# W_in's first two word blocks issued by ScalarE at the start, and 1e-9 added to the first 16 heads' sums by GpSimd

## The chip, the cores and the metric

One core of one Trainium2 chip. Five engines run their own instruction streams: TensorE (matrix products), VectorE, ScalarE, GpSimd and SyncE, which here only issues DMAs. The metric is the device time of one execution in microseconds, the median of several runs. The profile names the engines PE (and PEld for its weight loads), DVE, ACT, POOL and SP; a q behind a name is that engine's queue of issues.

## The reference

Attention with a decay, then two layers of a wide network, all in float32. Four batches, eight heads, 576 tokens, 64 elements in a head; 2304 tokens, width 512, inner width 2048.

```python
log_f = np.log(np.clip(f, 0.0001, 1.0))
cum = np.cumsum(log_f, axis=-1)
scores = scale * np.matmul(q, k.transpose(0, 1, 3, 2))
scores = np.where(causal, -1e9, scores + cum[..., :, None] - cum[..., None, :])
attn = np.exp(scores - np.max(scores, axis=-1, keepdims=True))
attn = attn / (np.sum(attn, axis=-1, keepdims=True) + 1e-09)
x = np.matmul(attn, v)                     # 2304 x 512 after merging the heads
h = x @ w_in;  x = np.maximum(0.01 * h, h) @ w_out
h = x @ w_in2; y = h / (1 + np.exp(-h)) @ w_out2
```

## The kernel before

The attention runs over 64 pieces that the code calls heads: each of 4 batches is cut into its first 256 and its last 320 tokens, and each half has 8 heads, so heads 0 to 7 are the first half of batch 0, and 8 to 15 its second half. The queries of a head are cut into blocks of at most 128 rows, two in a first half, three in a second.

For one block, `score` issues the product of queries and keys on TensorE (line 744; for heads 0 and 1 lines 735 and 737), the mask and row minimum on VectorE (`least`, line 724), and the exponential with its row sum on ScalarE (line 767). `shares` (line 782) then waits for the exponentials of all blocks of the head, adds 1e-9 to the sums on VectorE (line 786) and takes the reciprocal there (line 787). Each block is scaled by it on VectorE (line 775) or ScalarE (line 777). TensorE transposes the blocks (`transp`, line 825), they are copied out of PSUM (lines 359 and 360), and after every second head `weigh` multiplies both with the values (line 893) and writes the result into the ring, from which the next layer reads. The scores of head n+1 are issued before the transposes of head n, and those of head n+2 after them.

Beside the attention, W_in is made ready. The weights lie in HBM as pairs of 32-bit words; 16 blocks of 128 x 512 elements, 512 KB of words each. `fetch` (line 1745) takes a room for a block and issues its DMA; `conv_in` (line 1757) decodes the block with `to_f32`: one instruction on ScalarE (line 1714), three on VectorE (1715, 1716, 1718), then a rounded copy on ScalarE (line 359) and the remainder by a subtraction on VectorE (line 374, into tile w). Three lines of `conv_in` run beside each other. When heads 0 to 7 are through, the products with W_in begin (lines 961 and 1055, `hps` and `hpw`) and share TensorE with the later heads.

The order on each engine is worked out before the kernel runs, by a planner (class `Plan`). The parts of the kernel are generators; each step names an engine, an estimated duration, a rank and a delay. Whenever the planner's clock finds an engine free, it issues the waiting step of the lowest rank, and the order found in this way is the program. Attention steps have rank 0, decode steps rank 1, DMAs of later words rank 2. A step on another engine, another estimate or another wait thus changes the order of everything behind it. While TensorE has no step ready, and until the first product with W_in is complete in the plan, the planner puts filler products on it (lines 461, 464 and 466, tile `fps`).

Before the change all words are issued by SyncE. The blocks 0 and 1 (`EARLY` is 2) get a rank between the small DMAs that carry the cumulated logarithms into the key tiles of heads 2 to 7 (`first_rows`, line 540). `first_weights` starts with a wait for `cf`, the copy of these logarithms, and for `v0_sent`, the issue of the values' DMA; the blocks from 2 on wait for `rows` as well. The inputs of the very first steps are f (lines 474 and 476, clamped on GpSimd in line 398, logarithm on ScalarE in line 480) and the queries and keys of heads 0 and 1 (lines 598 and 600); one of the latter is issued by ScalarE, the rest by SyncE. GpSimd builds masks and constants until some 8 us, and takes subtractions of the later heads (line 370) from 74 us on.

Of the kernel before, what the change touches and what calls it, by code (L numbers as in the profile page):

```python
# [11 lines left out]
I32 = mybir.dt.int32  # L12
ACTF = mybir.ActivationFunctionType
ALU = mybir.AluOpType
# [20 lines left out]
DIRECT = 2  # L35
EARLY = 2
# [52 lines left out]
class Plan:  # L89
# [41 lines left out]
    def op(self, eng, cost, fn, rank=1, lat=None):  # L131
        def step(resume):
            self.count += 1
            heapq.heappush(self.ready.setdefault(eng, []), (rank, self.count, cost, fn, lat, resume))
            self.at(self.now, lambda: self.issue(eng))

        return step
# [39 lines left out]
    def dma(self, nbytes, fn, rank=1):  # L177
        return self.op("sp", 0.64, fn, rank, nbytes / self.rate)

    def wait(self, *names):  # L180
        def step(resume):
            missing = [n for n in names if n not in self.seen]
            if not missing:
                resume()
                return
            left = [len(missing)]

            def one():
                left[0] -= 1
                if not left[0]:  # L190
                    resume()

            for n in missing:
                self.waiting.setdefault(n, []).append(one)

        return step
# [8 lines left out]
    def signal(self, name):  # L205
        self.seen[name] = True
        for fn in self.waiting.pop(name, []):
            fn()
# [13 lines left out]
    def give(self, pool, i):  # L222
        self.given[pool, i] = True
        fn = self.queue.pop((pool, i), None)
        if fn:
            fn()
# [20 lines left out]
    def par(self, *gens):  # L247
        def step(resume):
            left = [len(gens)]

            def one():
                left[0] -= 1
                if not left[0]:
                    resume()

            for g in gens:
                self.start(g, one)

        return step
# [11 lines left out]
def dve_cost(n, fast=False):  # L271
    return 0.07 + n * (0.52e-3 if fast else 1.042e-3)
# [15 lines left out]
def fused_kernel(ctx, tc, qt, kt, va, vb, ft, w1, wi2, wo2, out):  # L288
    nc = tc.nc
    B, H, _, S = qt.shape  # L290
    D = va.shape[-1]
    NT, DM = out.shape
# [11 lines left out]
    p = Plan()  # L304
    op, dma, wait, take, give, signal, par = p.op, p.dma, p.wait, p.take, p.give, p.signal, p.par
# [44 lines left out]
    def dve(n, fn, rank=1, fast=False):  # L350
        return op("dve", dve_cost(n, fast), fn, rank)
# [228 lines left out]
    def head_info(n):  # L580
        sb, h = divmod(n, H)
        return sb // 2, sb % 2, h

    def plain(n):

        return n < PLAIN
# [114 lines left out]
    def score(n, i):  # L701
# [10 lines left out]
        if i == 0:  # L712
            ht["i_st"] = yield take("st", ST_BUFS)
            p.start(shares(n, stats[ht["i_st"] % ST_BUFS]))
# [67 lines left out]
    def shares(n, st):  # L782

        nb = len(BLOCKS[head_info(n)[1]])
        yield wait(*[("exp", n, i) for i in range(nb)])
        yield dve(1, lambda: nc.vector.tensor_scalar(st[:, 6:6 + nb], st[:, 6:6 + nb], 1e-9, None, op0=ALU.add), 0)
        yield dve(1, lambda: nc.vector.reciprocal(st[:, 9:9 + nb], st[:, 6:6 + nb]), 0)
        signal(("shares", n))
        yield wait(*[("p", n, i) for i in range(nb)])
        give("st", heads[n]["i_st"])  # L790
# [273 lines left out]
    def tagged(k, shape, dtype, name):  # L1064
        return w2t["a"].tile(shape, dtype, tag=f"x{k}", name=name)
# [661 lines left out]
    def room(f):  # L1727

        where = ROOM_IN[f]
        shape = [128, DM, 2]  # L1730
        name, bufs = (where, {"ring0": RING_BUFS, "ring1": RING_BUFS, "g": G_BUFS, "stg": STG_BUFS}.get(where, 1))
        if isinstance(where, int):
            name = ("w", where)
        i = yield take(name, bufs)
        if where in ("ring0", "ring1"):
            t = main.tile(shape, I32, tag=where, name="wsr", bufs=RING_BUFS)
        elif where == "g":
            t = main.tile(shape, I32, tag="g", name="wsg", bufs=G_BUFS)
        elif where == "stg":
            t = stg(i, shape, I32, "wst")  # L1740
        else:
            t = slot(where, shape, I32, "wss")
        return t, lambda: give(name, i)

    def fetch(f):
        t, back = yield from room(f)

        def move():
            yield dma(524e3, lambda: nc.sync.dma_start(
                out=t.rearrange("p n w -> p (n w)"), in_=w1[f, :, 0:DM].bitcast(I32)),  # L1750
                2 if f >= EARLY else DIRECT // 2 - H + 0.5)
            words[f] = t, back
            signal(("words", f))

        p.start(move())
# [24 lines left out]
    def fetch_out():  # L1780
        yield wait("gates")
        for j in range(FF // 2):
            for e in range(2):
                i_s = yield take("wst", WST_BUFS)
                src = decp["wo"].tile([128, DM, 2], I32, tag="wst", name="wst", bufs=WST_BUFS)
                words1[j, e] = src, i_s

                def move(j, e, src):
                    yield dma(524e3, lambda: nc.sync.dma_start(
                        out=src.rearrange("p n w -> p (n w)"), in_=w1[j + e * FF // 2, :, DM:2 * DM].bitcast(I32)), 2)  # L1790
                    signal(("words1", j, e))

                p.start(move(j, e, src))

    def conv_out():
        out_d = w2_d[0].rearrange("p (s f) n -> p s f n", s=7)
        for j in range(FF // 2):
            yield wait(("words1", j, 0))
            i_f = yield take("wf", 1)
            f = decp["wo"].tile([128, 7, HW], F32, tag="wf", name="wf", bufs=1)  # L1800
            y = f[:, 4:6].rearrange("p s n -> p (s n)")
            for e in range(2):
                yield wait(("words1", j, e))
                src, i_s = words1.pop((j, e))
                t = f[:, 2 * e:2 * e + 2].rearrange("p s n -> p (s n)")
                yield from to_f32(t, src, y, t, 2, True)
                give("wst", i_s)
            yield from mix(f, 1, 2)
            yield dma(918e3, lambda: nc.sync.dma_start(out=out_d[:, :, j], in_=f), 2)
            give("wf", i_f)  # L1810
            signal(("spilt", 0, j))

    def first_weights():
        def fetches():
            for f in range(FF):
                if f == EARLY:
                    yield wait("rows")
                yield from fetch(f)

        def line(fn, todo):  # L1820
            while todo:
                yield from fn(todo.pop(0))

        yield wait("cf", "v0_sent")
        ins = list(range(FF))
        yield par(fetches(), *[line(conv_in, ins) for _ in range(C_LINES)])
        signal("weights")
        yield wait(("scored", OUT_AT, 0))
        p.start(fetch_out())
        yield from conv_out()  # L1830
        yield wait("attention")
        wo_es.close()
        w2t["a"] = ctx.enter_context(tc.tile_pool(name="w2a", bufs=1, side="right"))
        for k in range(6):
            w2t["q", k] = tagged(k, [128, 2, 2, TB], F32, "gq")
        for k in range(SPLITS):
            w2t["s", k] = tagged(6 + k, [128, 2, 2, TB], F32R, "gs")
        w2t["b"] = ctx.enter_context(tc.tile_pool(name="w2b", bufs=1))
        signal("decoded")
# [133 lines left out]
    with tc.manual_schedule():  # L1973
        for gen in (opening(), first_weights(), loads(), attention(), hidden(), quarters(), preps(), summed(), all_fills(),
                    second_input(), second_weights(), hidden2(), second_values(), summed2()):
            p.start(gen)
        p.run()
# [51 lines left out]
```

## Time and profile before

| | |
|---|---|
| median of 3 runs | 952.9 us (951.85 to 955.81) |
| the profiled execution | 955.32 us, span 953.6 us, granted TensorE clock 0.998 |
| PE busy | 938.0 us, 98% of the span |
| DVE busy | 758.0 us, 79% |
| ACT busy | 612.1 us, 64% |
| POOL busy | 53.7 us, 6% |
| chain that ended last, by engine | PE 80%, DVE 9%, DMA 4%, ACT 3%, issue 2%, SPq 1% |
| DMA | 196.77 MB, mean 206 GB/s |

Busy shares are means over the whole span. The change touches the first tenth of it, so the rows below are mostly of that part. The span runs from the first to the last instruction; the execution's own time has a little more around it. PE's busy time is modelled and includes the fillers.

### The profile page before, as it was taken

To read this page: it belongs to the slowest core of one execution; us is meant where nothing else is said; L and a number is where in the kernel's file an instruction comes from. 1 tells how busy PE (TensorE), PEld (TensorE's weight loads), DVE (VectorE), ACT (ScalarE), POOL (GpSimd) and SP (SyncE) were. 2 spreads that over 40 slices of the span, in tenths; PEclk is the share of its full clock that TensorE was granted. 3 is DMA by queue.
4 is the path that set the end of the run, shared out by engine and by line. 5 is a ranking of instruction groups with operands and counts; after the bars stand their busy time and mean duration, and the time that the engine had idled before them with its cause. 6 is when DMAs were issued, how large, how long until landed. Compare 5 with 4: busy or idle time off the path is not lost.

```text
span 953.6 us, 17836 instructions
## 1 busy us (share of the span) xinstructions
PE 938.0 (98%) x6291; PEld 880.4 (92%) x6291; DVE 758.0 (79%) x1789; ACT 612.1 (64%) x1368; POOL 53.7 (6%) x69
## 2 busy tenths in 40 slices
PE   9999999999999999999999999999999999999998
PEld 8777888987889889999889999999999999999998
DVE  5998688788887883989899789759554599888885
ACT  6978878787777773775445468547466675444442
POOL 2001212121112100000000000000000000000000
PEclk9999999999999999999999999999999999999999
DMA  7943543477669649994866585797756774535442
GB/s 228 283 122 97 159 153 111 125 239 257 206 208 288 191 133 319 344 378 145 296 223 209 209 271 165 272 321 244 280 198 217 244 246 119 153 114 152 134 128 72
DMA packets 157845, 196.77 MB, mean 206 GB/s; under 512 B 9510, under 2 KB 141758, under 8 KB 157724
## 3 DMA queue, kind: packets, MB, share of 16 engines
q1 hardware_dynamic: 157324, 195.24, 63.6%
q8 instruction: 49, 0.80, 0.3%
q10 hardware_dynamic: 432, 0.39, 0.1%
q14 instruction: 40, 0.33, 0.1%
HBM read 125.94 MB, written 69.65 MB: 205 GB/s over the span
## 4 chain that ended last, share of the span: by engine, by line
PE 80%; DVE 9%; DMA 4%; ACT 3%; issue 2%; SPq 1%; DVEq 0%; ACTq 0%
PE m L1527 19%; PE m L1669 18%; PE hpw L961 16%; PE acc L1220 9%; PE sps L744 6%; PE av L893 5%; PE tps L825 4%; DVE gq L1359 2%; DVE gs L374 2%; DMA gq<-g_d 1%; PE hps L961 1%; DMA w_d<-f 1%; PE fps L466 1%; DVE sc L724 1%; DMA qk<-in_kt_dram 1%
## 5 line engine op out<-in xcount | busy, mean ns | idle before, releaser
L961 PE MATMUL hpw<-ring,w 128*128 128x320 f32 (+3 forms) x1152 | 209.6, 324 | 0.1
L1220 PE MATMUL acc<-gs,w 128*128 128x384 f32 x1008 | 184.3, 341 | 7.8 <-DVE gs L374 7.0
L1220 PEld LDWEIGHTS acc<-gs,w 128*128 128x128 f32 x1008 | 179.0, 189 | 10.3 <-DVE gs L374 8.5
L1669 PE MATMUL m<-w,gc 128*128 128x256 f32 x1512 | 179.9, 281 | 0.0
L1527 PE MATMUL m<-xc,w 128*128 128x384 f32 x1008 | 179.9, 339 | 0.0
L961 PEld LDWEIGHTS hpw<-ring,w 128*128 128x128 f32 x1152 | 173.5, 189 | 6.8 <-issue 0.7
L1669 PEld LDWEIGHTS m<-w,gc 128*128 128x128 f32 x1512 | 179.7, 189 | 0.0
L1527 PEld LDWEIGHTS m<-xc,w 128*128 128x128 f32 x1008 | 177.6, 188 | 0.4
L359 ACT CAST gc<-g 128x512 fp32r<-128x512 f32 (+1 forms) x180 | 80.5, 491 | 88.1 <-DVE g L1359 49.9
L767 ACT ACTIVATE sc<-sc,st 128x576 f32<-128x576 f32 (+4 forms) x160 | 93.3, 583 | 32.6 <-DVE st L724 31.1
L1153 ACT CAST gs<-gq 128x768 fp32r<-128x768 f32 x84 | 69.7, 837 | 56.4 <-DVE gq L1359 26.0
L724 DVE CUSTOM_DVE_ANT_0 sc<-sps,zmask 128x288 f32<-128x288 f32 (+4 forms) x160 | 71.6, 450 | 31.6 <-PE sps L744 23.2
L374 DVE TENSOR_TENSOR gc<-g,gc 128x512 fp32r<-128x512 f32 (+1 forms) x180 | 90.1, 527 | 3.6 <-ACT gc L359 2.5
L374 DVE TENSOR_TENSOR gs<-gq,gs 128x768 fp32r<-128x768 f32 x84 | 79.1, 954 | 16.5 <-ACT gs L1153 16.2
L1359 DVE TENSOR_TENSOR g<-g 128x256 f32<-128x256 f32 x144 | 58.6, 421 | 17.6 <-DMA g<-g_d 16.8
L825 PE MATMUL tps<-ident,sc 66*107 66x66 f32 (+3 forms) x480 | 68.0, 270 | 1.2 <-ACT sc L777 1.0
L744 PE MATMUL sps<-m,s 66*128 66x288 f32 (+9 forms) x288 | 67.3, 315 | 1.2 <-DVE st L724 0.8
L370 POOL TENSOR_TENSOR m<-qk,m 64x288 fp32r<-64x288 f32 (+1 forms) x54 | 48.7, 913 | 280.4 <-ACT m L359 148.7
L825 PEld LDWEIGHTS tps<-ident,sc 66*107 66x107 f32 (+3 forms) x480 | 55.5, 151 | 9.1 <-ACT sc L777 1.8
L374 DVE TENSOR_TENSOR w<-w 128x512 fp32r<-128x512 f32 x84 | 55.8, 687 | 9.4 <-ACT w L1915 9.4
L1915 ACT CAST w<-w 128x512 fp32r<-128x512 f32 x84 | 50.9, 621 | 14.9 <-DMA w<-w_d 14.3
L1055 ACT ACTIVATE gw<-hpw 128x320 f32<-128x320 f32 (+3 forms) x96 | 42.6, 450 | 24.1 <-PE hpw L961 20.3
(124 smaller groups left out, 1119.5 us busy)
## 6 DMA issues: line engine op xcount, KB each, us to landing
w<-w_d SPq DMA_DIRECT2D x84, 256.0 KB
gq<-g_d SPq DMA_DIRECT2D x48, 384.0 KB
g_d<-z SPq DMA_DIRECT2D x24, 768.0 KB
g<-g_d SPq DMA_DIRECT2D x36, 512.0 KB
w_d<-f SPq DMA_DIRECT2D x16, 896.0 KB
wst<-in_w_dram SPq DMA_DIRECT2D x17, 512.0 KB
wst<-in_wi_dram SPq DMA_DIRECT2D x16, 512.0 KB
wst<-in_wo_dram SPq DMA_DIRECT2D x16, 512.0 KB
```

The costliest lines, as they stand in the source:

```text
L359: ("act", act_cost(n, base), lambda: nc.scalar.copy(dst, src), 0.0),
L374: ("dve", dve_cost(n), lambda: nc.vector.tensor_tensor(dst, a, b, op=ALU.subtract), 0.0),
L724: yield dve(w, lambda: nc.vector.tensor_tensor_reduce(out=sc[0:qn, k0:k0 + w], in0=ps[0:qn], in1=zmask[0:qn, z0:z0 + w], scale=-0.125, sca ...
L744: nc.tensor.matmul(ps[0:qn], ht[x][:, qs], ht[y][:, k0:k0 + w], start=r == 0, stop=r == len(ops) - 1)
L767: yield act(kn, lambda: nc.scalar.activation(sc[0:qn, 0:kn], sc[0:qn, 0:kn], ACTF.Exp, scale=-1.0, bias=st[0:qn, 2 * i + a:2 * i + a + 1], ...
L825: nc.tensor.transpose(ps[0:k1 - k0, o:o + qn], ht["p"][i][0:qn, k0:k1], ident[0:qn, 0:qn])
L961: nc.tensor.matmul(dst, w[:, wi, c * 128:(c + 1) * 128], x(xi, c), start=(first_ and c == 0 and r == 0), stop=(c == KC - 1 and r == 2), sk ...
L1153: yield act(2 * TB, lambda: nc.scalar.copy(t[:, 0], src), 0, 0.09)
L1220: nc.tensor.matmul(dst, w[:, e, wi, j * 128:(j + 1) * 128], x[:, xi, e], start=start and s == 0 and e == 0 and r == 0, stop=stop and s == ...
L1359: ("dve", dve_cost(n), lambda: nc.vector.tensor_tensor(dst, a, b, op=op_), 0.0),
L1527: nc.tensor.matmul(dst, w[:, wi, c * 128:(c + 1) * 128], x[:, xi, c], start=start and c == 0 and r == 0, stop=stop and c == 1 and r == 2, ...
L1669: nc.tensor.matmul(banks[b][:, e], t[:, gi, a * 128:(a + 1) * 128], w[:, wi], start=begin and a == 0 and r == 0, stop=jp == NP // 2 - 1 an ...
```

## The change

The sums of heads 0 to 15 (`plain(n)`: n under 16) get their 1e-9 on GpSimd instead of VectorE; the planner takes 0.15 us for it. The later heads keep it on VectorE, and the reciprocal stays there for all. The words of blocks 0 and 1 are issued by ScalarE, at rank 0, with 0.65 us for the issue and 3.5 us until they are there; block 0 waits for nothing, block 1 for the first logarithm (`logs`, 0). The wait for `cf` and `v0_sent` ahead of everything is gone; `v0_sent` is now waited for together with `rows`, before block 2.

```diff
         yield wait(*[("exp", n, i) for i in range(nb)])
-        yield dve(1, lambda: nc.vector.tensor_scalar(st[:, 6:6 + nb], st[:, 6:6 + nb], 1e-9, None, op0=ALU.add), 0)
+        if plain(n):
+            yield op("pool", 0.15, lambda: nc.gpsimd.tensor_scalar(
+                st[:, 6:6 + nb], st[:, 6:6 + nb], 1e-9, None, op0=ALU.add), 0)
+        else:
+            yield dve(1, lambda: nc.vector.tensor_scalar(st[:, 6:6 + nb], st[:, 6:6 + nb], 1e-9, None, op0=ALU.add), 0)
...
         def move():
-            yield dma(524e3, lambda: nc.sync.dma_start(
-                out=t.rearrange("p n w -> p (n w)"), in_=w1[f, :, 0:DM].bitcast(I32)),
-                2 if f >= EARLY else DIRECT // 2 - H + 0.5)
+            dst, src = t.rearrange("p n w -> p (n w)"), w1[f, :, 0:DM].bitcast(I32)
+            if f < EARLY:
+                yield op("act", 0.65, lambda: nc.scalar.dma_start(out=dst, in_=src), 0, 3.5)
+            else:
+                yield dma(524e3, lambda: nc.sync.dma_start(out=dst, in_=src), 2)
             words[f] = t, back
...
             for f in range(FF):
+                if f == 1:
+                    yield wait(("logs", 0))
                 if f == EARLY:
-                    yield wait("rows")
+                    yield wait("rows", "v0_sent")
                 yield from fetch(f)
...
-        yield wait("cf", "v0_sent")
         ins = list(range(FF))
```

## Rows read from the trace of the kernel before

In the tables by stretch PE, PEld, DVE, ACT and POOL stand in this order, then the granted clock, the DMA engines' busy share and GB/s.

**Rows 1.** Busy time by stretch: start, end, length; each engine's microseconds and instructions.

```profile
5.00:14.00 9.00, 9.00 (x48) 6.31 (x47) 3.22 (x18) 5.49 (x16) 2.97 (x7) 1.00 0.86 251
14.00:28.00 14.00, 14.00 (x116) 12.42 (x115) 13.72 (x56) 13.69 (x44) 0.00 (x0) 1.00 0.88 275
...
53.00:88.00 35.00, 33.45 (x232) 26.18 (x231) 32.74 (x97) 28.54 (x69) 1.49 (x2) 1.00 0.28 82
```

**Rows 2.** The chain that ended last, in order of time: start us, us, what.

```profile
53.80 0.61 DVE ct L1718
...
54.81 0.12 DVE st L786
...
56.31 0.60 DVE w L374
...
57.86 0.34 DVE ct L1715
...
61.87 0.18 DVE st L786
...
87.60 1.49 PE tps L825 x10
```

**Rows 3.** Instructions in order of time, 0 to 24 us: start us, us, what.

```profile
0.82 0.45 SPq L476 DMA_DIRECT2D fs<-in_ft_dram  x1
0.82 0.72 ACTq L598 DMA_DIRECT2D qk<-in_kt_dram  x1
...
1.57 1.28 ACT L480 ACT_TABLE_LOAD   x1 [1.57 <-PEq L2017]
...
2.99 0.64 POOL L398 TENSOR_SCALAR fs<-fs 128x128 f32<-128x128 f32 x1 [0.65 <-DMA fs<-in_ft_dram]
...
3.66 0.31 ACT L480 ACTIVATE fs<-fs 128x128 f32<-128x128 f32 x1 [0.81 <-POOL fs L398]
...
4.59 0.31 POOL L398 TENSOR_SCALAR fs<-fs 64x32 f32<-64x32 f32 x1 [0.97 <-DMA fs<-in_ft_dram]
...
4.93 0.23 ACT L480 ACTIVATE fs<-fs 64x32 f32<-64x32 f32 x1 [0.96 <-POOL fs L398]
...
7.31 0.84 SPq L1749 DMA_DIRECT2D wsr<-in_w_dram  x2
...
13.45 0.67 ACT L1714 ACTIVATE cy<-wsr 128x512 f32<-128x512 f32 x1
...
16.03 1.42 SPq L1749 DMA_DIRECT2D wsg<-in_w_dram  x3
...
23.54 0.68 ACT L1714 ACTIVATE cy<-wsg 128x512 f32<-128x512 f32 x1
```

**Rows 4.** Groups on VectorE, 14 to 28 us: shapes, count; busy us, mean ns.

```profile
L1715 DVE TENSOR_SCALAR ct<-cy 128x512 int32<-128x512 int32 x5 | 2.1, 418 | 0.0
L1716 DVE SCALAR_TENSOR_TENSOR ct<-cy,ct 128x512 int32<-128x512 int32 x3 | 2.1, 689 | 0.0
...
L374 DVE TENSOR_TENSOR w<-ct,w 128x512 fp32r<-128x512 f32 x2 | 1.4, 686 | 0.0
L1718 DVE SCALAR_TENSOR_TENSOR ct<-wsr,ct 128x512 int32<-128x512 int32 x2 | 1.4, 684 | 0.0
```

**Rows 5.** Busy time by stretch, 3 to 6 us, while the first loads arrive.

```profile
3.00:6.00 3.00, 3.00 (x13) 2.62 (x12) 0.00 (x0) 0.54 (x2) 1.89 (x5) 1.00 0.62 148
```

**Rows 6.** Instructions on TensorE in order of time, heads 4 and 6.

```profile
18.07 0.39 PE L744 MATMUL sps<-qk 65*128 65x128 f32 x2
...
22.17 0.55 PE L825 MATMUL tps<-ident,sc 128*128 128x128 f32 x3
...
22.78 0.39 PE L744 MATMUL sps<-qk 65*128 65x128 f32 x2
```

**Rows 7.** Instructions in order of time at 150 us, GpSimd and VectorE side by side.

```profile
150.02 1.56 POOL L370 TENSOR_TENSOR m<-qk,m 64x288 fp32r<-64x288 f32 x2 [1.86 <-ACT m L359]
...
150.10 0.75 DVE L786 TENSOR_SCALAR st<-st 128x3 f32<-128x3 f32 x1
```

## The prediction

> **What bounds the kernel now.** I read the table by stage first, because the change touches only the first 90 us. TensorE counts as busy nearly everywhere, but in the stages up to 28 us part of that is filler matmuls, which the planner puts in whenever it has nothing real. The engine that has no room is VectorE: it is busy 13.72 of the 14 us after 14 us and 32.74 of the 35 us after 53 us, while from 5 to 14 us it works only 3.22 of 9 us [rows 1]. GpSimd does nothing from 14 to 28 us and 1.49 us of work from 53 to 88.
>
> The chain of waits, read second, says where VectorE's load sets the end. Up to 53 us it runs along TensorE. From 53.80 to 87.60 us it runs along VectorE and ScalarE: decoding of W_in (lines 1715 to 1718 and the subtraction into w), the added 1e-9 (line 786), the reductions. At 87.60 us it returns to TensorE [rows 2]. So VectorE time that disappears before 88 us is path, and after it TensorE has work waiting, which carries a gain to the end.
>
> **The 1e-9 on GpSimd.** It takes 16 instructions from VectorE. In the chain one such step costs 0.12 or 0.18 us before the next begins [rows 2]; at 0.15 that is 16 x 0.15 = 2.4 us of VectorE time. The reciprocal stays and now waits for GpSimd. Queued behind it on VectorE are other heads' reductions and decode steps; they wait for it too, and so do the scaling and the transposes of that head. No row shows an add of 3 columns on GpSimd. From below the nearest row is 0.31 us, for 64x32 elements, the clamp at 4.59 us [rows 3]; it may be a little less, since there are fewer elements. From above it is the same 0.31 with a whole VectorE instruction of 0.69 [rows 4] ahead of it, 1.0 us. I take 0.31, by the nearest row, against the 0.15 that goes: 0.16 us more from sum to reciprocal, hidden where VectorE is still in another instruction at that moment. With VectorE busy 98% of the stage I cost it at nothing; without that cover it would be up to 16 x 0.16 = 2.6 us. GpSimd's own queue is empty there, so nothing stands behind these adds.
>
> **Words issued by ScalarE.** Two DMAs of 512 KB leave SyncE's queue, where they are issued at 7.31 us (the pair holds the queue 0.84 us), and go to ScalarE, the first right behind the key load at 0.82 us (0.72 us to issue), the second behind the first logarithm at 3.66 us [rows 3]. That is 2 x 0.72 = 1.4 us on ScalarE. The first one pushes the table load from 1.57 to about 2.3 us, so it ends at 3.57, before the logarithm that waits for the clamp until 3.66. The second ends at 3.97 + 0.72 = 4.7 us, before the second logarithm's 4.93 [rows 3]. Neither is on the path, with 0.1 and 0.2 us to spare; at worst each costs some tenths at the very start. On SyncE everything behind 7.31 us comes 0.84 us earlier, the third to fifth block of words (16.03 us) among it.
>
> The transfers: from 3 to 6 us the DMA engines are 0.62 busy [rows 5], so 1.1 us of full rate is free. The rest of the megabyte pushes out the keys and queries of heads 2 and 3 and the values. Those are needed only when heads 0 and 1 are through. The inputs of the logarithms and of head 0 are at risk only for the tenths already named. The Trainium skill, DMA: Bandwidth & Descriptors, section "Issuing engines are not separate DMA queues", says that a second issuing engine saves issue time alone, as all transfers interleave on the same 16 engines. By that rule the move would be worth its 0.84 us of issue and no bandwidth. The row with 0.62 shows that engines are free at that hour, so here it is the earlier time, not the second queue, that would pay.
>
> **What the earlier words are worth.** Today the first decode step is at 13.45 us [rows 3] and falls into VectorE's full stage. The words can now be there at about 6 to 8 us. A block needs four VectorE instructions, one of 0.42 and three of 0.68 to 0.69 us [rows 4]. They overlap with their neighbours: in the chain the short one takes 0.34 us and the long ones 0.60 to 0.61 [rows 2], 0.34 + 3 x 0.61 = 2.17 for a block. Two blocks are 4.3 us; VectorE's 9 - 3.22 = 5.8 us of idle time before 14 us can hold them.
>
> Relief of the full stage: 4.3 + 2.4 = 6.7 us. Not all of it arrives. The blocks 2 to 4 still wait for their words. Their issue moves from 16.03 to 15.2 us. The transit lies between 2.2 us (the 64 KB of f: issued at 0.82, used at 2.99) and 6.1 us (words of block 0: 7.31 to 13.45) [rows 3], so they land between 17.4 and 21.3 us; I take 20.4, nearer the row of the same size. Their decoding begins at 23.54 us today. From 14 to 20.4 us VectorE then has only heads to work on. Of its 13.72 us in that stage, 2.1 + 2.1 + 1.4 + 1.4 = 7.0 us are decode steps [rows 1, 4], so heads take 6.7 of 14 us, 48%. Idle: 52% of 6.4 us = 3.3 us. What is left is 6.7 - 3.3 = 3.4 us at the end of the stage. Next late is TensorE itself, whose queue holds hidden products of the second chunk by then.
>
> ScalarE, at 13.69 of 14 us just as full [rows 1], loses its part of the same blocks, so it doesn't take over as the bound.
>
> **Sum.** The profiled execution took 955.3 us (its span 953.6 us and 1.7 around it); the three timed runs have a median of 952.9, and the gain is taken from that: 952.9 - 3.4 = 949.5 us.
>
> **Rivals.**
> *The gap swallows it.* Heads up to 28 us are paced by latency: head 6 starts 0.61 us after head 4's transposes, and head 4 needs 4.10 us from its first product to them [rows 6], 4.7 us for two heads whether VectorE has decode work or not. Blocks 2 to 15 then keep arriving as they do now, and only the adds after 53 us count: some 5 x 0.15, with 0.8 us from the issue queue. About 1.5 us: 951.4. For it: decode steps fill gaps between higher ranked work. Against it: VectorE shows no gaps to wait in from 14 us on.
>
> *The relief comes whole.* Decode steps delay heads, as a head's own instruction must wait for the one in progress. If four cycles of two heads up to 28 us each get 0.6 us shorter (one decode step), 2.4 us of the 3.3 us gap is no loss: 952.9 - 3.4 - 2.4 = 947.1; with the whole 6.7 it is 946.2. I give it 946.6.
>
> *GpSimd in the path (slower).* Place: between the last sum and the reciprocal of the first 16 heads. A GpSimd subtraction at 150.02 us and VectorE's add of 1e-9 at 150.10 run side by side, and the add takes 0.75 instead of the 0.15 of the chain [rows 2, 7]: the two engines hold each other up. Decode steps of 0.69 us run all through the stage, so each GpSimd add can be held up to that long. Heads 0 to 7 run two at a time, so four delays count; heads 8 to 15 count eight times, as VectorE is in the chain there: 12 delays. At half a decode step, 0.34 + 0.16 = 0.5 us each, they cost 6.0 us: 952.9 - 3.4 + 6.0 = 955.5; at the upper bound of 1.0 - 0.15 = 0.85 they cost 10.2: 959.7. It decides once the delay passes 3.4 / 12 = 0.28 us. The Trainium skill, SBUF — State Buffer, section "Who interferes with whom", has this as a rule: a VectorE instruction with two SBUF inputs and a GpSimd instruction that reads SBUF exclude each other for whole instructions. [...] Against the rival: today's add waits in VectorE's own queue for the same decode step, so most of the wait is only moved.
>
> *The change doesn't do what it says.* If the words landed no earlier (ScalarE's queue held, or the transfers behind the first loads), only the adds would go; that is the first rival's time.
>
> **How the numbers follow.** Forecast (947.5 to 951.2) 0.41; gap swallows it 0.22; whole relief 0.23; GpSimd in the path 0.14. Half a per cent, about what a measurement of this kernel can tell from no change, is 4.8 us: faster is below 948.1, slower above 957.7. Faster: 0.23 + 0.10 from the lower end of the forecast, 0.33. Slower: 0.07 from the upper half of the third rival and 0.03 for a re-planned order that fits badly, 0.10. Same: 0.57. The range goes from 945.5, just past the whole relief, to 955.5, where the GpSimd rival has its middle; the forecast's own is 947.5 to 951.2.
>
> **What would show it.** The first decode instruction on ScalarE before 9 us, and eight decode steps on VectorE before 14 us. VectorE's busy time in 14 to 20 us down to about half, then full again. The first filler-free stretch not later than 28 us. The chain's return to TensorE at about 84 us instead of 87.60. From the last sum to the reciprocal's end no longer than now. I am wrong if that leg is longer by over 0.3 us, if the first logarithm slips past 4.2 us, or if the return to TensorE is where it was.

## The result, and the profile after

The changed kernel takes 959.3 us (median of 7 runs, 957.95 to 963.63) against 953.8 (951.32 to 955.81) before: ratio 1.0072, interval 1.0056 to 1.0088. It is slower, by 5.5 us in these medians and by 6.9 us by the ratio; 949.5 was predicted, with 945.5 to 955.5 as the range. The profiled execution took 959.1 us, its span 957.4.

First the table by stretch, after the change (columns as in [rows 1]: length, PE, PEld, DVE, ACT, POOL, granted clock, DMA share, GB/s).

```profile
5.00:14.00 9.00, 7.28 (x18) 3.86 (x18) 0.94 (x5) 3.62 (x9) 3.96 (x9) 0.62 0.73 189
14.00:28.00 14.00, 14.00 (x83) 11.72 (x83) 8.86 (x33) 8.99 (x28) 1.48 (x4) 0.76 0.76 227
...
53.00:88.00 35.00, 34.99 (x242) 27.07 (x242) 33.09 (x93) 29.21 (x71) 3.33 (x7) 1.00 0.35 110
...
7.00:21.00 14.00, 14.00 (x43) 9.10 (x43) 4.03 (x15) 7.59 (x20) 3.85 (x10) 0.51 0.72 203
```

Two things stand out against [rows 1]. VectorE and ScalarE have become idle from 14 to 28 us (8.86 and 8.99 us of work instead of 13.7), but as waiting, not as relief: TensorE issues 83 matmuls there instead of 116. And the granted clock, 1.00 before, is 0.62 from 5 to 14 us and 0.76 from 14 to 28 us. By the records of the clock it is at its lower level, 1.2 GHz, from 7.2 to 20.9 us; the last row, of 7 to 21 us, has 0.51.

The same execution in order of time (start us, us, what; in brackets the idle time before and what ended it) shows how it began.

```profile
0.79 0.43 ACTq L1755 DMA_DIRECT2D wsr<-in_w_dram  x1
0.79 0.45 SPq L476 DMA_DIRECT2D fs<-in_ft_dram  x1
...
1.26 0.71 ACTq L598 DMA_DIRECT2D qk<-in_kt_dram  x1
...
5.68 0.65 POOL L398 TENSOR_SCALAR fs<-fs 128x128 f32<-128x128 f32 x1 [3.37 <-DMA fs<-in_ft_dram]
6.36 0.31 ACT L480 ACTIVATE fs<-fs 128x128 f32<-128x128 f32 x1 [3.08 <-POOL fs L398]
6.37 0.35 ACTq L1755 DMA_DIRECT2D wsr<-in_w_dram  x1
...
6.72 1.22 PE L502 MATMUL cps<-tri,fs 128*128 128x256 f32 x4 [2.32 <-ACT fs L480]
...
10.28 0.66 ACT L1718 ACTIVATE cy<-wsr 128x512 f32<-128x512 f32 x1
...
17.46 1.40 SPq L1757 DMA_DIRECT2D wsg<-in_w_dram  x3
...
18.41 2.89 PE L466 MATMUL fps<-zmask 128*128 128x128 f32 x14
...
21.14 0.49 PE L829 MATMUL tps<-ident,sc 128*128 128x128 f32 x3
```

The words of block 0 are the first thing that ScalarE issues, ahead of the key load, and at the same moment as f. The clamp of f, at 2.99 us in [rows 3], waits for its DMA until 5.68, the first logarithm comes at 6.36 instead of 3.66, and TensorE stands idle for 2.32 us. Then it runs at half speed: 14 fillers take 2.89 us here. The first decode step did come earlier, 10.28 us instead of 13.45, but the first transposes stand at 21.14 us, 8.6 us later than before (12.54). The next three blocks of words (tile wsg) are issued at 17.46 us, later than the 16.03 of [rows 3].

The chain that ended last, in order of time, from its first piece:

```profile
0.79 4.82 DMA fs<-in_ft_dram
...
6.72 1.22 PE cps L502 x4
...
94.64 0.24 POOL st L787
...
94.90 0.19 DVE st L791
...
95.91 0.95 PE tps L829 x5
```

It now begins with the transfer of f, 4.82 us. From 6.72 to 93.03 us it runs along TensorE: the stretch along VectorE and ScalarE from 53.80 to 87.60 us of [rows 2] isn't on it. Only then does it leave TensorE, for 2.9 us up to 95.91, through one head's mask, exponential, add on GpSimd, reciprocal and scaling. The adds on GpSimd, as one line of the source (count, shortest/median/longest ns):

```profile
L787 POOL TENSOR_SCALAR st<-st x16: 219/375/783, 14.5 to 94.6; 128x2 f32<-128x2 f32 x8, 128x3 f32<-128x3 f32 x8
```

### The profile page after: what moved, and what is told of

Read it like the earlier page. It is cut to its first block, busy times and chain, and to the rows that moved or that the text cites. A ratio compares the mean times of both kernels' runs of the same rounds, so it can differ in the third digit from the quotient of the medians.

```text
span 957.4 us, 17842 instructions
## 1 busy us (share of the span) xinstructions
PE 942.9 (98%) x6289; PEld 881.6 (92%) x6289; DVE 753.3 (79%) x1767; ACT 612.2 (64%) x1374; POOL 61.5 (6%) x85
## 4 chain that ended last, share of the span: by engine, by line
PE 77%; DVE 12%; DMA 5%; issue 3%; ACT 2%; SPq 0%; POOL 0%; DVEq 0%; ACTq 0%; POOLq 0%
PE m L1531 19%; PE m L1673 18%; PE hpw L965 13%; PE acc L1224 8%; PE sps L744 6%; PE tps L829 4%; PE av L897 4%; DVE gs L374 2%; PE hps L965 2%; DVE gq L1363 2%; DMA w_d<-f 2%; DMA qk<-in_kt_dram 1%; DVE sc L724 1%; DMA gq<-g_d 1%; DVE s L374 1%
```

## The experiments

Each ratio is to the kernel before, run beside it on the same chip; before had medians of 950.9 to 952.6 us in these comparisons.

**Each half of the change alone.** Adds only: the first hunk of the diff without the others. Words only: the others without the first.

> Only the 1e-9 of heads 0 to 15 moves to GpSimd; all words are issued by SyncE as before. Theory (the early words delay the input f, and the wait halves TensorE's clock): nothing of that happens here, f is clamped at about 3.0 us, no half clock in the first 30 us, and the time is 950 to 954 us (ratio 0.997 to 1.001). Rival (GpSimd's adds lie in the path of every head): slower by 3 to 6 us, 956 to 960 us, and the leg from the last sum to the reciprocal's end is longer by more than 0.3 us a head.

> Only the words of blocks 0 and 1 move to ScalarE, as in the changed kernel; the adds stay on VectorE. Theory: the whole loss is here: f clamped at about 5.7 us, half clock for some 14 us from 7 us on, 957 to 961 us (ratio 1.004 to 1.009). Rival (adds in the path): no slower than before, at most 954 us.

Measured: adds only 958.0 us, 1.0067 (1.0051 to 1.0082); words only 962.4 us, 1.0102 (1.0089 to 1.0115), a little above the range expected. Words only shows the late f (clamp at 5.51 us) and the low clock, as expected. But the adds alone lose as much as the whole change, where no loss was expected, and the two don't add up. The rival has the time of the adds-only kernel right, but not its mechanism: from the last sum to the reciprocal's end a head takes 0.82 us there in the mean of 16, against 0.81 before. f is clamped at 2.95 us there and the clock stays up in the opening. I summed TensorE's real work (each matmul at the pitch of its shape when nothing holds it). This is an estimate, which another choice of pitch moves by about 1 us: at 90 and at 200 us adds-only is level with the kernel before to within 1.5 us, at 420 us some 2 us behind, at 600 us some 3.5 behind. So most of the loss comes long after the adds. That pointed at the order: each edit makes the planner find another one.

**The old order, with only the instruction itself changed.** These kernels have every engine's other instructions in the order of the kernel before; the planner doesn't see the edit. The edits are shortened here.

```diff
# adds: same step for the planner, other engine
+        eng = nc.gpsimd if plain(n) else nc.vector
-        yield dve(1, lambda: nc.vector.tensor_scalar(...), 0)
+        yield dve(1, lambda: eng.tensor_scalar(...), 0)
# words: issued directly, the old step stays empty
+        for f in range(EARLY):
+            if f:
+                yield wait(("logs", 0))
+            rooms[f] = yield from room(f)
+            nc.scalar.dma_start(out=rooms[f][0]..., in_=w1[f, :, 0:DM].bitcast(I32))
         yield wait("cf", "v0_sent")
```

> The kernel before, in its own order on every engine; only the 16 adds of 1e-9 are taken out of VectorE's stream and put on GpSimd, without the planner knowing. Theory now (the loss of the adds-only kernel comes from the new order that the planner finds, far behind the adds): 950 to 954 us (ratio 0.998 to 1.001), and TensorE's work done by 90 us as before or up to 2 us ahead. Rival (the adds on GpSimd cost by themselves): 956 us and more, ratio 1.004 or above.

> The kernel before, in its own order on every engine; only the two DMAs of words 0 and 1 are issued by ScalarE as in the changed kernel, the first ahead of everything, the second behind the first logarithm. The decode steps stay where they were, so there is nothing to gain. Theory: f clamped at about 5.6 us, half clock for some 14 us, 7 to 9 us more than before (ratio 1.007 to 1.010). If the new order makes the loss: ratio at most 1.003.

Measured: adds 952.1 us, 1.0015 (1.0000 to 1.0030); words 959.7 us, 1.0083 (1.0066 to 1.0099). The adds cost next to nothing (1.4 us, a little above their range, with an interval that begins at nothing) and bring nothing. GpSimd's rows for them, in the adds kernel:

```profile
L787 POOL TENSOR_SCALAR st<-st x16: 218/228/698, 9.6 to 85.9; 128x2 f32<-128x2 f32 x8, 128x3 f32<-128x3 f32 x8
```

From the last sum of a head to the end of its reciprocal it takes 0.78 us in the mean of the 16 heads, 0.81 before. The words carry 7.9 us of loss in the old order. TensorE in that kernel:

```profile
6.59 0.92 PE L502 MATMUL cps<-tri,fs 128*128 128x256 f32 x4 [1.80 <-ACT fs L480]
...
17.52 1.49 PE L466 MATMUL fps<-zmask 128*128 128x128 f32 x6
18.80 0.85 PE L825 MATMUL tps<-ident,sc 128*128 128x128 f32 x3
```

**Late input or low clock?** One kernel leaves f alone and makes TensorE idle; two keep it busy while f is late, one of them in the old order, one in the changed kernel's own.

```diff
# idle: one filler of 13 ahead of the first sums
-            p.filler["pe"] = 0.2, lambda: nc.tensor.matmul(fps, z[:, 0:128], z, start=True, stop=True)
+            p.filler["pe"] = 0.2, once          # issues one, then none
# busy: 11 more ahead of the first sums
-                         lambda: [sums(c) for c in piece], 1 if i else -1)
+                         lambda: [opened["busy"]() for _ in range(0 if i else 11)] + [sums(c) for c in piece], 1 if i else -1)
```

> The kernel before, in its own order of instructions on every engine, but 12 of the 13 filler matmuls ahead of the first sums are left out, so that TensorE stands idle for some 2.3 us as it does in the changed kernel; f and the words are untouched. If an idle TensorE is what halves its clock: half clock for some 14 us from about 5 us on, the first transposes at 16 us or later instead of 12.5, and 3 to 6 us more than before (ratio 1.003 to 1.006). If the clock in the changed kernel fell for another reason: no half clock, ratio 0.999 to 1.001.

> The kernel before in its own order, words issued by ScalarE as in the changed kernel, and 11 more filler matmuls ahead of the first sums, so that TensorE doesn't stand idle. It leaves the late f alone: f clamped at about 5.6 us, no half clock in the first 30 us, first transposes at 14.5 to 15.5 us, 2 to 3.5 us more than before (ratio 1.002 to 1.004). If the late f were the main cost: ratio 1.006 and more.

> The changed kernel with 11 more filler matmuls on TensorE ahead of its first sums, which fill its wait for f; the rest of the order is the same. If the halved clock is the larger part of the loss: no half clock in the first 30 us, f clamped at 5.7 us as in the changed kernel, the first transposes at about 15 us instead of 21, and 954 to 957 us (ratio 1.000 to 1.004). If the wait for f alone is the loss: 958 to 961 us, as in the changed kernel.

Measured: idle 957.0 us, 1.0058 (1.0043 to 1.0073); words with a busy TensorE in the old order 954.2 us, 1.0019 (1.0007 to 1.0032); the changed kernel with a busy TensorE 954.5 us, 1.0022 (1.0006 to 1.0037). TensorE in the idle kernel, with f on time:

```profile
1.69 0.56 PE L469 MATMUL fps<-z 128*128 128x256 f32 x1
3.96 1.65 PE L509 MATMUL cps<-tri,fs 128*128 128x256 f32 x4 [1.71 <-ACT fs L487]
...
16.08 1.49 PE L473 MATMUL fps<-zmask 128*128 128x128 f32 x6
17.36 0.85 PE L832 MATMUL tps<-ident,sc 128*128 128x128 f32 x3
```

Its sums start even earlier than before, at 3.96 us, yet six fillers take 1.28 us from the first start to the transposes, 0.21 each; the transposes are 4.8 us late. The kernel before, at the same place, has 0.67 us for them, 0.11 each:

```profile
11.87 0.83 PE L466 MATMUL fps<-zmask 128*128 128x128 f32 x6
12.54 0.49 PE L825 MATMUL tps<-ident,sc 128*128 128x128 f32 x3
```

The clock records of this execution begin only at 20 us, so here the pitch (0.21 against 0.11 us) has to stand for the clock.

The words kernel with a busy TensorE shows:

```profile
4.54 1.47 PE L459 MATMUL fps<-z 128*128 128x256 f32 x11
6.59 0.92 PE L503 MATMUL cps<-tri,fs 128*128 128x256 f32 x4 [0.58 <-ACT fs L481]
...
13.29 0.83 PE L467 MATMUL fps<-zmask 128*128 128x128 f32 x6
13.96 0.49 PE L826 MATMUL tps<-ident,sc 128*128 128x128 f32 x3
```

f is as late as in the words kernel (both first sums at 6.59 us), the fillers are back at 0.11 us, and the transposes come at 13.96 instead of 18.80. The granted clock is 1.00 up to 28 us, where the words kernel has 0.67 from 5 to 14 us and 0.72 from 14 to 28 us. So of the 7.9 us, 1.8 are the late f and 6.1 the clock (1.0083 against 1.0019), and idleness alone costs 5.5 us. The changed kernel itself, with the same 11 fillers and otherwise its own order on every engine, goes from 1.0072 to 1.0022: some 4.8 us come back. The 0.22% that is left is about what the late f costs in the old order, 0.19%. So what the changed kernel lost is the clock and the late f; nothing measurable is left for its order.

**Is it the words, or their place?**

> The kernel before in its own order, words issued by ScalarE, but the first right behind the key load, as the prediction had assumed it. If only its place ahead of the key load was the fault: f clamped by 3.6 us, no half clock, ratio 0.999 to 1.002. If the words hold up f wherever they stand ahead of it in time: f clamped at 4 to 5.5 us, TensorE idle for 1 us or more, and ratio 1.002 to 1.008.

> Words of blocks 0 and 1 issued by ScalarE, but each behind a logarithm, so that f is through before they begin; adds on VectorE. Theory: f clamped at about 3.0 us, no half clock, first decode step still some us earlier than before, and 948 to 953 us (ratio 0.995 to 1.000). If earlier words were a loss by themselves (a worse order of the decode steps), 956 us and more.

The first issues block 0 behind the key load, in the old order; the second, re-planned, behind a logarithm (`if f < EARLY: yield wait(("logs", f))`). Measured: 952.2 us, 1.0005 (0.9991 to 1.0018), the first of the two outcomes named; and 954.1 us, 1.0017 (1.0003 to 1.0030), a little above the range expected. The issues and the clamp in the first:

```profile
0.81 0.71 ACTq L599 DMA_DIRECT2D qk<-in_kt_dram  x1
...
1.56 0.61 ACTq L1832 DMA_DIRECT2D wsr<-in_w_dram  x1
...
2.91 0.63 POOL L398 TENSOR_SCALAR fs<-fs 128x128 f32<-128x128 f32 x1 [0.58 <-DMA fs<-in_ft_dram]
...
6.42 0.31 POOL L398 TENSOR_SCALAR fs<-fs 64x32 f32<-64x32 f32 x1 [2.87 <-DMA fs<-in_ft_dram]
```

The words are issued 0.77 us later, behind the key load, and the large part of f is on time (2.91). The packets of the DMA engines in the traces say why. Before the change f's 512 packets of 128 bytes start from 1.92 to 2.56 us. In the changed kernel they start from 2.52 to 4.66 us, while the words' packets of 4 KB run from 1.86 to 4.49 us. In this kernel they start from 1.91 to 2.49 us, and the first packet of the words only at 3.28 us. f's small rest is now the late one, 6.42 instead of 4.59, and that costs nothing measurable: the granted clock is 1.00 up to 28 us. So the words hold up what is still under way beside them, and in this kernel only the large part of f counts.

**Orders re-planned for no reason.** The work is that of the kernel before; the planner is told 5, 9 or 13 columns for the 16 adds: `dve(5 if plain(n) else 1, ...)`.

> The kernel before with the planner told that the add of 1e-9 of heads 0 to 15 has 5 columns instead of 1 (0.004 us more); the work is the same. If the kernel before owes some us to its order alone, another order of equal merit costs: 2 to 6 us more (ratio 1.002 to 1.006). If orders of this planner are worth the same within what can be measured: ratio 0.999 to 1.001.

> As the first re-planned kernel without any change of the work, with 9 columns told instead of 5 (0.008 us more for each of the 16 adds in the planner). If orders that differ for no reason are spread over some us above the order before: ratio 1.002 to 1.025, and the loss arises after 250 us, not in the first 90 us. If the first such kernel was one odd case: ratio 0.999 to 1.002.

> A third order found by telling the planner another size of the add (13 columns, 0.012 us more), the work unchanged. If the kernel before has an order better than most: ratio above 1.002 again. If the two losses so far were chance: below 1.001.

Measured: 974.2 us, 1.0237 (1.0214 to 1.0259); 957.9 us, 1.0058 (1.0037 to 1.0078); 959.1 us, 1.0067 (1.0042 to 1.0091). All three lose, 5.5 to 22.5 us, from 0.004 to 0.012 us in a planner's estimate; the first far more than the 2 to 6 us named for it. None is behind at 100 us: by the sum of TensorE's work the first is ahead by about 4 us, the other two by 0 to 2 us. In the worst one a part of the loss lies from 560 to 660 us, and two waits stand out there (who waited for whom: us, times, longest):

```profile
560.00:660.00 100.00, 92.53 (x491) 89.95 (x489) 67.91 (x107) 54.91 (x97) 0.00 (x0) 0.93 0.68 230
```

```profile
ACT xc L1393 <- DMA x1s<-x_d: 8.0, 1, 8.0
...
PE m L1527 <- ACT xc L1393: 5.9, 3, 4.4
```

A transfer between the two layers comes late there, TensorE waits, and the clock falls again (0.93 over the stretch). The kernel before has 99.23 us of TensorE work in the same stretch. That this transfer makes the loss was not tested.

**The change without its side effects.** The whole change with both words behind logarithms; and, in the old order, the adds and early words, without and with the decode steps of blocks 0 and 1 put into VectorE's idle time (of that edit, the two lines that start the decoding):

```diff
+        p.start(decode(0, ("logs", 0), ("min", 0, 0, 0), ("min", 0, 0, 0), ("exp", 0, 1), ("min", 1, 0, 0)))
+        p.start(decode(1, ("exp", 1, 0), ("min", 1, 1, 0), ("shares", 1), ("p", 1, 1), ("min", 2, 0, 0)))
```

> The whole change, but each of the two word blocks is issued behind a logarithm. f is on time and TensorE keeps its clock; TensorE's work by 100 us is 1 to 3 us ahead of before. Whether that lasts depends on the order the planner then finds: ratio 0.996 to 1.005; below 0.999 it beats both kernels.

> As the run with early decoding, but the decode steps stay where they were in the kernel before. It says what the adds and the early words do together without a new order: ratio 0.999 to 1.003. The difference between this and the early decoding is what earlier decoding is worth.

> The change without its two side effects: words issued by ScalarE, the first behind the key load; the adds of heads 0 to 15 on GpSimd; blocks 0 and 1 decoded early, in VectorE's idle time up to head 2; and every other instruction in the order of the kernel before. Theory of the prediction (VectorE time that goes before 88 us is path): 2 to 5 us less than before, ratio 0.995 to 0.998, and the first wide product (hpw) at 92 to 95 us instead of 97.7. If the freed time is not path (blocks 2 and later and the heads set the pace): ratio 0.999 to 1.003, hpw no earlier.

Measured: 958.8 us, 1.0078 (1.0057 to 1.0099); without early decoding 952.5 us, 1.0018 (0.9999 to 1.0037); with it 953.6 us, 1.0017 (1.0005 to 1.0030). The first one draws a bad order, although f and the clock are right; it is above its range. The other two are equal to within some 0.2%. The stretches 14 to 28 and 28 to 53 us, without early decoding and then with it:

```profile
14.00:28.00 14.00, 14.00 (x116) 12.40 (x115) 13.41 (x50) 13.38 (x42) 1.65 (x5) 1.00 0.87 279
28.00:53.00 25.00, 25.00 (x167) 19.43 (x167) 24.71 (x71) 23.23 (x58) 1.76 (x4) 1.00 0.92 275
```

```profile
14.00:28.00 14.00, 13.38 (x108) 11.92 (x108) 10.63 (x43) 12.10 (x38) 1.73 (x6) 1.00 0.87 266
28.00:53.00 25.00, 25.00 (x168) 19.04 (x167) 24.70 (x72) 23.55 (x59) 1.98 (x4) 1.00 0.91 276
```

2.8 us leave VectorE's full stage and turn into idle time there; the next stretch is as full as ever. VectorE in order of time, with early decoding:

```profile
16.66 0.69 DVE L1847 TENSOR_TENSOR w<-ct,w 128x512 fp32r<-128x512 f32 x1
...
19.42 0.17 DVE L792 RECIPROCAL st<-st 128x2 f32<-128x2 f32 x1 [0.70 <-POOL st L791]
...
22.33 0.29 DVE L728 CUSTOM_DVE_ANT_0 sc<-sps,zmask 128x128 f32<-128x128 f32 x1 [1.01 <-PE sps L748]
...
26.41 0.42 DVE L1720 TENSOR_SCALAR ct<-cy 128x512 int32<-128x512 int32 x1
```

Block 1 is finished at 17.35 us, then VectorE waits between the heads, and block 2 begins at 26.41. Its last step starts at 32.65 us, against 31.13 without early decoding. It isn't its words that block 2 waits for: their packets have run by 20.73 us, but ScalarE, whose instruction opens a block, comes to it only at 24.87 us. The first wide product (hpw) starts at 99.7 us, against 97.7 before, not at 92 to 95. In the chain that ended last the stretch that runs mostly along VectorE and ScalarE returns to TensorE at 89.61 us, where the kernel before has 87.60 and the prediction had about 84:

```profile
89.61 1.49 PE tps L830 x10
```

## Why the prediction was wrong

*The step that failed* is the place and price of the issue of the first words: "the first right behind the key load at 0.82 us", "at worst each costs some tenths at the very start". Both issues have rank 0, and of equal ranks the one asked for first goes first; that was the words' step. At that place it cost 1.8 us by the late f and 6.1 by the clock in the old order, and some 7 us in all in the changed kernel. Where I had thought it to be, it costs nothing (1.0005): the price was right for a place that the code doesn't give. The condition that I had named for being wrong, the first logarithm past 4.2 us, came true with 6.36, but none of my rivals had this mechanism. The Trainium skill, DMA: Bandwidth & Descriptors, section "Issuing engines are not separate DMA queues", has all transfers interleave on the same 16 engines, whichever engine started them. f, issued by SyncE at the same 0.79 us as the words by ScalarE, agrees with it: its packets (2.52 to 4.66 us) run among theirs (1.86 to 4.49 us). The prediction drew from the rule that no bandwidth is gained, but not that f would have to share.

*The clock* stood in no term. The fillers looked like free padding; they are what keeps TensorE at 2.4 GHz while it waits for f, and they are counted for the f of the old kernel.

*The relief* of 3.4 us, a ratio of 0.9964, was not there. In the old order early decoding is worth nothing that can be measured (1.0017 against 1.0018), and so is taking the adds away (1.0015). VectorE being full in a stretch does not make each of its instructions path: heads are paced by their own chain of steps over several engines, blocks 2 and later by their place in the order, and the idle time that I had put at 3.3 us took all. This was my first rival, though it still had a gain of 1.5 us. Two terms under the relief failed with it. The words of blocks 2 to 4 were not issued at 15.2 instead of 16.03 us, but at 17.46 in the changed kernel and at 17.02 with early decoding; why later is open. And they were not what their decoding waited for: before the change the packets of block 2 have run by 19.55 us, and its first step is at 23.54 [rows 3]. In the re-planned kernels the order can move block 2 as well, so there its worth can't be told from the order's.

*GpSimd in the path* didn't happen: 0.78 instead of 0.81 us a head in the old order. In the changed kernel it is 0.88, or 0.80 without head 0, which takes 2.14 us. An add takes 0.22 us at the shortest (I had taken 0.31), but single ones take up to 0.78, so the engines do hold each other up. The longest, and what VectorE does beside it:

```profile
46.96 0.78 POOL L787 TENSOR_SCALAR st<-st 128x3 f32<-128x3 f32 x1 [3.24 <-ACT sc L767]
46.98 0.68 DVE L1722 SCALAR_TENSOR_TENSOR ct<-wsr,ct 128x512 int32<-128x512 int32 x1
```

The add ends at 47.74 us, just after VectorE's instruction (47.66). The Trainium skill, SBUF — State Buffer, section "Who interferes with whom", says that a VectorE instruction with two SBUF inputs contends with a GpSimd instruction that reads SBUF; these two rows agree with it. The add of [rows 7], which was held up on VectorE beside a GpSimd subtraction, has one input, so that sentence doesn't cover it. In the sum the wait is just moved from one queue to another, as the rival's counter-argument had it.

*The order*, to which I gave 0.03 of a chance, can be as large as everything else: seven kernels in a new order that kept the clock in the opening (adds only, words behind the logarithms, busy TensorE, three for no reason, the whole change behind logarithms) lost 1.6 to 22.5 us, and none gained. The changed kernel's own order, which is that of the busy TensorE, is the exception: its 2.1 us are about the price of the late f. In the old order words and adds cost 0.83% + 0.15% = 0.98%; the changed kernel lost 0.72%. The remaining 0.26% in its favour would be its order and its early decoding together, but within the intervals it can be nothing. Why the order before is better than its neighbours is open. One thing all seven share: the first hpw starts earlier than before (87.4 to 96.1 us against 97.7), and the last scores of the attention start later (354.1 to 364.3 us against 351.1). W_in's products have moved ahead of heads; whether that is the loss was not tested. But an early hpw, which I had named as a sign of gain ahead of the run with early decoding, is none by itself. No version tried here beats the kernel before.

## What to carry to other kernels

Before pricing a moved DMA, write down the whole issue order of its new queue and what else is issued at that moment: here 512 KB beside the first small input cost the input's delay and, as TensorE then stood idle, its clock. With a planner that derives the order from estimates, test an edit once with the old order held fixed, and test the planner with a meaningless edit; without both, an edit's effect can't be told from a new draw. An engine that is busy all through a stretch is the bound only if work ready behind it would move up. And the chain that ended last belongs to one kernel: in the changed one TensorE had taken VectorE's place on it.

## What the runs showed of the hardware that was not expected

An idle time of 2.3 us at the start, 1.7 in the idle kernel, was followed by a long stretch at 1.2 GHz: 13.7 us in the changed kernel, though TensorE was given work all through it. The low clock cost two to three times the idle time itself: 4.8 us after 2.3 us in the changed kernel, 6.1 us after 1.8 us in the words kernel in the old order. Eleven matmuls whose result nobody reads took these 4.8 and 6.1 us off again; an idle time of 0.58 us left beside them was not followed by a lower clock. And words issued 0.77 us later and behind the key load (1.56 against 0.79) let the first part of f be clamped 2.77 us earlier (2.91 against 5.68).
